# Fourier mixing and squared-ReLU MLP on one core: mirrored columns of the first sequence joined in the second block, small tables on ScalarE's queue, another order of folding and products

## The chip, the cores and the metric

The kernel runs on one core of a Trainium2 chip. The metric is the time of one execution on the device in microseconds; lower is better. It is given as the median of several runs, and one further execution is recorded by the hardware profiler.

## The reference, cut to what matters

```python
# x: (8, 3008, 256) float32; w_in: (256, 2048), w_out: (2048, 256)
X = np.fft.fft(np.fft.fft(x, axis=1), axis=2).real      # along the sequence, then along the features
h = X.reshape(24064, 256) @ w_in
g = np.maximum(h, 0.0) ** 2
out = g @ w_out
```

There are eight sequences of 3008 rows. Each goes through a two-dimensional Fourier transform whose real part is kept, and then through a two-layer network with a squared ReLU between the layers.

## The kernel before, in words

**The two halves of the work.** The transform along the features is folded into the first weight matrix: `G1` (cosines times `w_in`) and `G2` (sines times `w_in`) are made once, piece by piece, by `begin_win` and the two matmuls of L315. What is left per sequence is the transform along its 3008 rows. It gives two matrices with one column per frequency, `Pt` (cosine part) and `Qt` (sine part), and a row `Et` for the one feature column that fits in neither. The main loop then walks over blocks of 251 frequencies (`CK`) and, within a block, over eight steps `j`: `front` multiplies `Pt` and `Qt` by `G1` and `G2` (L838, L839), joins them on VectorE (L841, L843, L844), `combine` squares on ScalarE, and `back` multiplies by `w_out`. The first eight steps (the first block) also convert the weights, the second eight make sums of `w_out` (`sum_wout`). From step 8 on GpSimd forms sums for `back`.

**The first sequence** has no earlier steps to hide in, so it is transformed in a first phase ahead of the loop, in an order written out by hand. That phase is what the change is about. Its stages:

- *Load.* Seven tiles `xt` of the input (numbers 0 to 6) and the tables `cosT` and `sinT` come from memory. Tiles 0 and 1 use small tables of 95 columns, tiles 2 and 3 small tables of 189 columns, tiles 4 to 6 (`ODD0` on) large ones of 377 columns for each parity. A small table takes several DMAs. `load_table` and `load_x` issue all of these on SP's queue. `load` brings a piece of `w_in` or `w_out` as raw 64-bit words.
- *Fold.* VectorE folds each tile in two halves: `for_p(t)` (L485, L501, L515) for the cosine part, `for_q(t)` (L489, L505, L515) for the sine part. `for_p` also has ScalarE copy one column into `lone` (`f_e`, L518), which lies in the buffer `wsum`.
- *Products.* TensorE multiplies the folded tiles by the tables (L632). There are three kinds, each for both parities `kp`: P (`w` by `cosT`, into `Pt`), E (`lone` by `cosT`, for the lone column) and Q (`w` by `sinT`); E and Q add into the same PSUM tiles. The products of tiles 0 to 3 are called even, those of 4 to 6 odd.
- *Join.* ScalarE copies a part of the even products out of PSUM (`copy_4`, L650, tile `da`), and VectorE joins them in two rounds (`join_4`, `join_2`) and then with the odd products: `join_lo` gives frequencies 0 to 752, `join_hi` the mirrored ones, 753 to 1504. `join_1` does both. For Q and E these joins are the ones of L669 and L671.
- *Hand over.* `spread_e` takes the last row of `Qt` and spreads its first 251 values over all partitions by a matmul (L816); `spread_rest` does the other 1254 by two DMAs on GpSimd's queue. `copy_e` scales a column of `G2` to `gE`.

`awake(n)` issues n matmuls (L228) on a spare tile `filled`, whose result nobody uses.

**What sets the order.** The kernel is written under a manual schedule: every engine works through its own instructions in the order in which the code issues them. Each transfer issued by SP or ScalarE raises one of eight counters when it has landed. [...]

Of the kernel before, what the change touches and what calls it, by code (L numbers as in the profile page):

```python
# [8 lines left out]
F32 = mybir.dt.float32  # L9
U32 = mybir.dt.uint32  # L10
AF = mybir.ActivationFunctionType
ALU = mybir.AluOpType
# [70 lines left out]
def kernel(  # L83
# [108 lines left out]
    G2 = const.tile([P, F], F32, name="G2")  # L192
    gE = const.tile([P, NFC], F32, name="gE")

    def load_table(tab, src, tiles):

        for t in tiles:
            c, r0, step, rows = TILES[t]
            for i, (s0, count) in enumerate(row_tiles(S)):
                mine = [r for r in range(count) if (s0 + r - r0) % step == 0 and 0 <= (s0 + r - r0) // step < rows]  # L200
                if mine:
                    o, m = (s0 + mine[0] - r0) // step, len(mine)
                    while m % 15 and m % 16 and o + m < P and mine[0] + step * m < P:
                        m += 1
                    nk = NC[0][c]
                    nc.sync.dma_start(out=tab[o:o + m, :, PLACE[t]:PLACE[t] + nk],  # L206
                                     in_=src[mine[0]:mine[0] + step * (m - 1) + 1:step, :, i, 0:nk])

    make_identity(nc, ident)
    last = ident[:, P - 1:]  # L210
# [394 lines left out]
    def dft_ops(b):  # L605
# [7 lines left out]
        def group(kp, which):  # L613
# [6 lines left out]
            def product(ps, c, lone_e=False, only=None):  # L620

                ts = [t for t in range(NT) if TILES[t][0] == c]
                for t in ts if only is None else ts[only:only + 1]:
                    rows = TILES[t][3]
                    if b is None:
                        w = we[0:rows, SPOT[t], kp]
                    elif lone_e:
                        w = lone[0:rows, 2 * t + kp]
                    else:
                        w = folded[b, t][0:rows, kp, PART[which]]  # L630
                        w = w if which else w[:, 0:n]
                    nc.tensor.matmul(ps[0:w.shape[-1]], w,  # L632
                                     (cosT if lone_e else tab)[0:rows, kp, PLACE[t]:PLACE[t] + NC[kp][c]],
                                     start=t == ts[0] and (lone_e or not both_in), stop=t == ts[-1] and not lone_e,
                                     skip_group_check=both_in)
# [12 lines left out]
            def copy_4():  # L648
                a = st["a"] = hp.tile([P, 2 * P], F32, name="da", tag="da", bufs=2)[0:n]
                nc.scalar.copy(a[:, 0:n2], st["ps"][0:n, 0:n2])  # L650

            def even_part(c, lone_e):

                if c == 0 and lone_e == both_in:
                    pool, tag = (psm, ("mC", "mD")[kp]) if both_in else (psd, "d")
                    st["ps"] = pool.tile([P, 512], F32, name="pd", tag=tag)
                at, nk = EVEN[c][1:]
                product(st["ps"][:, at:at + nk], c, lone_e)
                if c == 2 and not lone_e:
                    copy_4()  # L660

            def both(lo, hi, a, ps, only=None):

                nk, nh = a.shape[-1], hi.shape[-1]
                if both_in:

                    join = nc.vector.scalar_tensor_tensor
                    if only != 1:
                        join(out=lo, in0=ps, scalar=signs[:, 0:1], in1=a, op0=ALU.mult, op1=ALU.add)  # L669
                    if only != 0:  # L670
                        join(out=hi[:, ::-1], in0=a[:, 0:nh], scalar=signs[:, 1:2], in1=ps[:, 0:nh],  # L671
                             op0=ALU.mult, op1=ALU.add)
                    return
                tt(out=lo, in0=a, in1=ps, op=ALU.add)
                if which == 1:
                    tt(out=hi[:, ::-1], in0=ps[:, 0:nh], in1=a[:, 0:nh], op=ALU.subtract)
                else:
                    tt(out=hi[:, ::-1], in0=a[:, 0:nh], in1=ps[:, 0:nh], op=ALU.subtract)

            def join_4():  # L680
                a, ps = st["a"], st["ps"]
# [2 lines left out]

            def join_2():
                a, ps = st["b"], st["ps"]
                st["c"] = hp.tile([P, NC[0][3]], F32, name="dc2", tag="dc2", bufs=2)[0:n, 0:n0]
                both(st["c"][:, 0:n1], st["c"][:, n1:n0], a, st["half"] if b != 0 else ps[:, 2 * n2:2 * n2 + n1])

            def odd_part(i, lone_e):  # L690
# [93 lines left out]
                     st["odd"], only)  # L784

            if b == 0:
                named = [("join_4", join_4), ("join_2", join_2), ("lo", join_lo), ("hi", join_hi),
                         ("join_1", join_1)]
                for i in range(3):
                    for nm, f in (("even", even_part), ("odd", odd_part)):  # L790
                        named += [(nm + ("", "_e")[e] + str(i), lambda i=i, e=e, f=f: f(i, e == 1)) for e in range(2)]
                return [((which, kp, nm), f) for nm, f in named]
            ops = [(0.0, even_n), (0.5, join_4), (0.7, join_2), (0.0, odd_n), (1.1, join_1)]
            from_psum.update((join_4, join_2, join_turned))
# [21 lines left out]
        nc.tensor.matmul(ps, last.to_broadcast([P, P]), qt[:, 0:CK], start=True, stop=True)  # L816
        nc.scalar.copy(et[:, 0:CK], ps)

    def spread_rest():
        _, qt, et = PQE[0]  # L820
        nc.gpsimd.dma_start(out=e_dram[0:1], in_=qt[P - 1:P])
        nc.gpsimd.dma_start(out=et[:, CK:], in_=e_dram[0:1, CK:].to_broadcast([P, NKT - CK]))

    def load_e(b):
        nc.sync.dma_start(out=PQE[b][2], in_=e_dram[b:b + 1].to_broadcast([P, NKT]))
# [184 lines left out]
    def for_p(t):  # L1010
        for i in (0, 2, 4):
            pieces[t][i]()
# [18 lines left out]
        product()  # L1031


    start()
    awake(48)
    for t in range(2):
        load_x(0, t)
    for_p(0)
    for_q(0)
    for_p(1)  # L1040
    begin_win(0)
    load_x(0, 2)
    load_x(0, 3)
    for dst, src in ((cosd, cos_d), (sind[:, :, 0:P - 1], sin_d), (sind[:, :, P - 1:], alt_d)):
        nc.sync.dma_start(out=dst, in_=src.rearrange("(c p) m -> p c m", p=P))
    load_table(cosT, cos_s, (0, 1))
    load_x(0, 4)
    load_x(0, 5)
    load_table(cosT, cos_s, (2, 3))
    load_x(0, 6)  # L1050
    load_table(cosT, cos_s, range(ODD0, NT))
    load_table(sinT, sin_s, range(ODD0, NT))
    win[1] = load(pair_in(1))
    load_table(sinT, sin_s, range(ODD0))
    win[2] = load(pair_in(2))
    for_p(2)
    rounded(0)
    win[0][1]()
    awake(2)
    for_p(3)  # L1060
    p_part("even0", "even1")
    q_part("even_e0", "even_e1")
    awake(6)
    p_part("even2")
    q_part("even_e2")
    for_q(1)
    for_p(4)
    for_p(5)
    for_q(2)
    for_p(6)  # L1070
    p_part("odd0", "odd1", "odd2")
    q_part("odd_e0", "odd_e1", "odd_e2")
    groups[0, 0, "join_4"]()
    groups[0, 0, "join_2"]()
    for_q(4)
    groups[0, 1, "join_4"]()
    groups[0, 1, "join_2"]()
    for_q(5)
    p_part("join_1")
    for_q(6)  # L1080
    q_part("odd0", "odd1", "odd2")
    copy_e = win[0][2]()
    begin_win(1)
    for_q(3)
    q_part("even0", "even1", "even2")
    awake(12)
    rounded(1)
    for kp in range(2):
        for nm in ("join_4", "join_2", "lo"):
            groups[1, kp, nm]()  # L1090
        if kp == 0:
            begin_win(2)
    spread_e()
    q_part("hi")
    copy_e()
    spread_rest()
    LAG = 2
    BLOCKS = [(k0, min(CK, NKT - k0)) for k0 in range(0, NKT, CK)]
    steps = [(b, k0, n, j) for b in range(B) for k0, n in BLOCKS for j in range(NJ)]
# [75 lines left out]
    for i in range(len(steps) + LAG + 4):  # L1175
        if i < len(steps):
            b, k0, n, j = steps[i]
            if i == NJ:
                for k in range(NX):
                    load_later(k)  # L1180
            if NJ <= i < NJ + NL:
                load_column(i - NJ)
            if i % per == 0:
                assert not side
                side = ahead(b + 1) if b + 1 < B else []
                spent, pace = 0.0, sum(t for t, _ in side) / sum(share(i + k) for k in range(per - 2))
            multiply()
            g = front(b, k0, n, j, between)
            if i < NJ:
                weights()  # L1190
                s = combine(n, g, True)
            elif i < 2 * NJ:
                if j < 4:
                    sum_wout(slice(j // 2 * (NJ // 2), (j // 2 + 1) * (NJ // 2)), j % 2)
        while finished and finished[0][0] <= i:
            store(*finished.pop(0)[1:])
        if i >= LAG and flight:
            at, g_, s_ = flight.pop(0)
            final = at[:3] == (B - 1, *BLOCKS[-1])
            back(at[2], at[3], g_, s_, final)  # L1200
            if at[3] == NJ - 1:
                c_ = gather(at[2], s_ is None, final)
                finished += [(i + 2 + s, *at[:3], s, c_, final) for s in range(2)]
        if i < NJ:
            copy_e = win[i + 1][2]() if i + 1 < NJ else None
            leftover()
            if copy_e:
                copy_e()
        if i < len(steps):
            flight.append(((b, k0, n, j), g, s if i < NJ else combine(n, g, False)))  # L1210
# [63 lines left out]
```

## Time and profile before

| | |
|---|---|
| median of 3 runs | 1921.69 us (1921.37 to 1922.04) |
| profiled execution, its own time | 1921.49 us |
| its span from first to last instruction | 1919.7 us |
| TensorE busy | 1908.8 us, 99% of the span |
| VectorE, GpSimd, ScalarE busy | 1444.8, 1121.0, 952.5 us |
| first matmul of the main loop (L838) | starts at 43.24 us |
| DMA moved before 33 us | 7.27 MB on SP's queue |

The span begins with the first instruction. All times below count from there. The first phase ends where L838 first appears in TensorE's timeline; all else is the loop. A duration on TensorE is that of a group in the timeline, in which each float32 matmul shows as two instructions.

### The profile page before, as it was taken

How to read it: one execution, taken by the hardware profiler on the slowest of the kernel's cores; microseconds unless marked ns; L12 is line 12 of the kernel's file. 1: busy time of each engine (PE TensorE's matmuls, PEld its weight loads, DVE VectorE, ACT ScalarE, POOL GpSimd, SP SyncE). 2: the span in 40 equal slices, each digit the busy share in tenths (PEclk: the TensorE clock that was granted, in tenths of full speed). 3: DMA queues.
4: the chain of work that ended last, by engine and by line, in shares of the span. 5: the costliest groups of instructions: out<-in, count | busy, mean ns of one | idle time of the engine just before them, and what ended most of it. 6: DMA issues, size and time to landing. Idle time of an engine off the chain costs nothing.

```text
span 1919.7 us, 28162 instructions
## 1 busy us (share of the span) xinstructions
PE 1908.8 (99%) x9270; PEld 1699.7 (89%) x9270; DVE 1444.8 (75%) x3646; ACT 952.5 (50%) x1201; POOL 1121.0 (58%) x1709
## 2 busy tenths in 40 slices
PE   9999999999999999999999999999999999999998
PEld 7888898888988898888988889888898888988887
DVE  8988887787687876788668876788767777655554
ACT  2755554555454554445545454455544555444444
POOL 0255655665566655665666665556655666566565
PEclk9999999999999999999999999999999999999999
DMA  7431211110011101111011100111001101100100
GB/s 213 129 33 33 54 30 36 28 42 17 28 36 41 34 12 35 30 45 28 12 36 42 41 21 12 47 36 36 22 20 45 36 12 22 28 12 12 22 11 23
DMA packets 146622, 69.58 MB, mean 36 GB/s; under 512 B 130145, under 2 KB 137259, under 8 KB 146474
## 3 DMA queue, kind: packets, MB, share of 16 engines
q1 hardware_dynamic: 146022, 66.87, 14.1%
q8 instruction: 73, 1.20, 0.3%
q14 instruction: 75, 0.61, 0.1%
q0 software_dynamic: 176, 0.65, 0.1%
q10 hardware_dynamic: 276, 0.26, 0.0%
HBM read 43.03 MB, written 24.69 MB: 35 GB/s over the span
## 4 chain that ended last, share of the span: by engine, by line
PE 96%; DVE 2%; DMA 1%; SPq 0%; ACT 0%; issue 0%; POOL 0%; DVEq 0%; ACTq 0%
PE ph L838 17%; PE ph L839 17%; PE mC L891 16%; PE mA L891 16%; PE mB L891 16%; PE mD L891 8%; PE pd L740 1%; PE pd L632 1%; PE mA L878 1%; PE mB L878 1%; PE pd L714 1%; DMA xt<-in_x_dram 1%; DMA cosT<-in_cos_s_dram 0%; PE pg L315 0%; SPq L206 0%
## 5 line engine op out<-in xcount | busy, mean ns | idle before, releaser
L853 ACT ACTIVATE g<-g 128x1004 f32<-128x1004 f32 (+1 forms) x384 | 399.0, 1039 | 691.8 <-DVE g L844 453.5
L841 DVE SCALAR_TENSOR_TENSOR he<-Et,gE,ph 128x251 f32<-128x251 f32 (+1 forms) x768 | 362.6, 472 | 343.2 <-PE ph L839 338.8
L861 POOL TENSOR_TENSOR s<-g 128x251 f32<-128x251 f32 (+1 forms) x376 | 236.7, 630 | 636.6 <-ACT g L854 576.7
L838 PE MATMUL ph<-Pt,G 128*128 128x251 f32 (+1 forms) x1536 | 452.5, 375 | 0.4 <-DVE g L844 0.3
L839 PE MATMUL ph<-Qt,G 127*128 127x251 f32 (+1 forms) x1536 | 451.3, 374 | 0.0
L854 ACT ACTIVATE g<-g 128x1004 f32<-128x1004 f32 (+1 forms) x384 | 399.3, 1040 | 12.2
L891 PE MATMUL mC<-s,wsum 128*128 128x251 f32 (+1 forms) x1504 | 381.4, 374 | 0.0
L891 PE MATMUL mA<-g,wout 128*128 128x251 f32 (+1 forms) x1504 | 380.1, 374 | 0.0
L843 DVE TENSOR_TENSOR g<-he,ph 128x251 f32<-128x251 f32 (+1 forms) x768 | 320.4, 417 | 53.5 <-POOL s L861 1.4
L839 PEld LDWEIGHTS ph<-Qt,G 127*128 127x128 f32 x1536 | 291.3, 190 | 35.7
L891 PEld LDWEIGHTS mC<-s,wsum 128*128 128x128 f32 x1504 | 285.5, 190 | 34.5
L838 PEld LDWEIGHTS ph<-Pt,G 128*128 128x128 f32 x1536 | 285.5, 189 | 34.5 <-DVE g L844 0.8
L844 DVE TENSOR_TENSOR g<-he,ph 128x251 f32<-128x251 f32 (+1 forms) x768 | 314.1, 409 | 0.0
L891 PEld LDWEIGHTS mA<-g,wout 128*128 128x128 f32 x1504 | 282.6, 189 | 35.3 <-issue 0.3
L862 POOL TENSOR_TENSOR s<-s,g 128x251 f32<-128x251 f32 (+1 forms) x376 | 270.7, 720 | 29.5
L863 POOL TENSOR_TENSOR s<-g 128x251 f32<-128x251 f32 (+1 forms) x376 | 272.4, 724 | 0.0
L864 POOL TENSOR_TENSOR s<-g,s 128x251 f32<-128x251 f32 (+1 forms) x376 | 241.9, 643 | 0.0
L891 PE MATMUL mB<-g,wsum 128*128 128x251 f32 (+1 forms) x752 | 220.5, 374 | 0.0
L891 PE MATMUL mD<-s,wout 128*128 128x251 f32 (+1 forms) x752 | 220.3, 374 | 0.0
L891 PE MATMUL mB<-s,wout 128*128 128x251 f32 (+1 forms) x752 | 219.9, 374 | 0.0
L891 PEld LDWEIGHTS mB<-g,wsum 128*128 128x128 f32 x752 | 142.6, 190 | 17.4
L891 PEld LDWEIGHTS mD<-s,wout 128*128 128x128 f32 x752 | 141.9, 189 | 17.7
(176 smaller groups left out, 1387.6 us busy)
## 6 DMA issues: line engine op xcount, KB each, us to landing
out_dram<-os SPq DMA_DIRECT2D x376, 56.0 KB
xt<-in_x_dram SPq DMA_DIRECT2D x39, 384.0 KB
xt<-in_x_dram SPq DMA_DIRECT2D x63, 128.0 KB
Et<-e_dram SPq DMA_DIRECT2D x7, 752.5 KB
out_dram<-os SPq DMA_DIRECT2D x288, 6.8 KB
raw<-in_moe_w_in_dram SPq DMA_DIRECT2D x16, 256.0 KB
raw<-in_moe_w_out_dram SPq DMA_DIRECT2D x16, 256.0 KB
xt<-in_x_dram SPq DMA_DIRECT2D x2, 512.0 KB
```

The lines of the kernel that those rows point to most:

```text
L838: nc.tensor.matmul(hP, G1[:, fs], pt[:, ks], start=True, stop=True)
L839: nc.tensor.matmul(hQ, G2[0:P - 1, fs], qt[0:P - 1, ks], start=True, stop=True)
L841: nc.vector.scalar_tensor_tensor(out=t, in0=et[:, ks], scalar=gE[:, fc:fc + 1], in1=hP, op0=ALU.mult, op1=ALU.add)
L843: tt(out=g[:, h, 0, 0:n], in0=t, in1=hQ, op=ALU.add)
L844: tt(out=g[:, h, 1, 0:n][:, ::-1], in0=t, in1=hQ, op=ALU.subtract)
L853: act(v, v, AF.Relu)
L854: act(v, v, AF.Square)
L861: gt(out=s1, in0=g21, in1=g22, op=ALU.add)
L862: gt(out=s2, in0=s1, in1=g11, op=ALU.subtract)
L863: gt(out=s3, in0=g11, in1=g21, op=ALU.subtract)
L864: gt(out=s4, in0=g12, in1=s2, op=ALU.subtract)
L891: nc.tensor.matmul(acc[nm][:, i, 0:n], w, v[:, 0:n], start=j == 0 and i == 0, stop=j == NJ - 1, skip_group_check=True)
```

## The change

1. `load_table` takes a queue. The small tables of `cosT` (tiles 0 to 3) and `sinT` (tiles 0 to 3) are issued by ScalarE, in three places of its order; the large ones stay on SP, which issues all seven tiles of the input ahead of them. A one-element copy on ScalarE stands first.
2. The order of folds and products is new: the P products of tiles 0 and 1 come ahead of the first `G1`/`G2` matmuls, with `awake(26)` between; the E products of tiles 5 and 6 and the Q products come later. Before the hand-over stands `awake(24)` in place of `awake(12)`.
3. Only `join_lo` is done in the first phase. `keep` copies the odd products of P and Q out of PSUM on ScalarE, into tiles of the pool `wp`, and the four `join_hi` run in steps 8 to 11, one a step.
4. The second conversion of `w_in` (`begin_win(1, True)`) has its last product on GpSimd and not on VectorE.
5. The row of `Et` is spread in two parts: frequencies 251 to 752 early on GpSimd's queue (`spread_lower`), the rest in steps 9 and 11 by SP (`store_upper`, `load_upper`).

```diff
 
-    def load_table(tab, src, tiles):
+    def load_table(tab, src, tiles, queue=nc.sync):
...
-                    nc.sync.dma_start(out=tab[o:o + m, :, PLACE[t]:PLACE[t] + nk],
-                                     in_=src[mine[0]:mine[0] + step * (m - 1) + 1:step, :, i, 0:nk])
+                    queue.dma_start(out=tab[o:o + m, :, PLACE[t]:PLACE[t] + nk],
+                                    in_=src[mine[0]:mine[0] + step * (m - 1) + 1:step, :, i, 0:nk])
...
-            def even_part(c, lone_e):
+            def even_part(c, lone_e, only=None):
...
-                product(st["ps"][:, at:at + nk], c, lone_e)
-                if c == 2 and not lone_e:
-                    copy_4()
+                product(st["ps"][:, at:at + nk], c, lone_e, only)
...
-                tt(out=lo, in0=a, in1=ps, op=ALU.add)
+                if only != 1:
+                    tt(out=lo, in0=a, in1=ps, op=ALU.add)
+                if only == 0:
+                    return
...
+            def held_w():
+                return wp.tile([P, 2, D], F32, name="w", tag="w").rearrange("p a d -> p (a d)")[0:n, 0:n0]
+
+            def keep():
+                o = held_w()
+                nc.scalar.copy(o, st["odd"])
+                st["odd"] = o
+
...
-                st["c"] = hp.tile([P, NC[0][3]], F32, name="dc2", tag="dc2", bufs=2)[0:n, 0:n0]
+                st["c"] = held_w() if both_in else hp.tile([P, NC[0][3]], F32, name="dc2", tag="dc2", bufs=2)[0:n, 0:n0]
...
         nc.scalar.copy(et[:, 0:CK], ps)
 
-    def spread_rest():
+    KH = S // 4 + 1
+
+    def spread_lower():
         _, qt, et = PQE[0]
-        nc.gpsimd.dma_start(out=e_dram[0:1], in_=qt[P - 1:P])
-        nc.gpsimd.dma_start(out=et[:, CK:], in_=e_dram[0:1, CK:].to_broadcast([P, NKT - CK]))
+        nc.gpsimd.dma_start(out=e_dram[0:1, 0:KH], in_=qt[P - 1:P, 0:KH])
+        nc.gpsimd.dma_start(out=et[:, CK:KH], in_=e_dram[0:1, CK:KH].to_broadcast([P, KH - CK]))
+
+    def store_upper():
+        nc.sync.dma_start(out=e_dram[0:1, KH:], in_=PQE[0][1][P - 1:P, KH:])
+
+    def load_upper():
+        nc.sync.dma_start(out=PQE[0][2][:, KH:], in_=e_dram[0:1, KH:].to_broadcast([P, NKT - KH]))
...
+    def folds_of(names):
+        for nm in names.split():
+            (for_p if nm[0] == "P" else for_q)(int(nm[1:]))
+
+    def products_of(names):
+        for nm in names.split():
+            (p_part if nm[0] == "P" else q_part)({"P": "", "Q": "", "E": "e"}[nm[0]] + nm[1:])
+
     start()
     awake(48)
-    for t in range(2):
-        load_x(0, t)
-    for_p(0)
-    for_q(0)
-    for_p(1)
+    load_x(0, 0)
+    load_x(0, 1)
+    nc.scalar.copy(turn[0:1, 0, 0:1], ident[0:1, 0:1])
+    load_table(cosT, cos_s, (0, 1), nc.scalar)
+    folds_of("P0 Q0 P1")
     begin_win(0)
     load_x(0, 2)
     load_x(0, 3)
     for dst, src in ((cosd, cos_d), (sind[:, :, 0:P - 1], sin_d), (sind[:, :, P - 1:], alt_d)):
         nc.sync.dma_start(out=dst, in_=src.rearrange("(c p) m -> p c m", p=P))
-    load_table(cosT, cos_s, (0, 1))
-    load_x(0, 4)
-    load_x(0, 5)
-    load_table(cosT, cos_s, (2, 3))
-    load_x(0, 6)
+    for t in range(ODD0, NT):
+        load_x(0, t)
+    load_table(cosT, cos_s, (TWO, TWO + 1), nc.scalar)
     load_table(cosT, cos_s, range(ODD0, NT))
+    win[1] = load(pair_in(1))
     load_table(sinT, sin_s, range(ODD0, NT))
-    win[1] = load(pair_in(1))
-    load_table(sinT, sin_s, range(ODD0))
     win[2] = load(pair_in(2))
-    for_p(2)
+    folds_of("Q1 P2")
     rounded(0)
+    products_of("P0 P1")
+    awake(26)
     win[0][1]()
-    awake(2)
-    for_p(3)
-    p_part("even0", "even1")
-    q_part("even_e0", "even_e1")
-    awake(6)
-    p_part("even2")
-    q_part("even_e2")
-    for_q(1)
-    for_p(4)
-    for_p(5)
-    for_q(2)
-    for_p(6)
-    p_part("odd0", "odd1", "odd2")
-    q_part("odd_e0", "odd_e1", "odd_e2")
-    groups[0, 0, "join_4"]()
-    groups[0, 0, "join_2"]()
-    for_q(4)
-    groups[0, 1, "join_4"]()
-    groups[0, 1, "join_2"]()
-    for_q(5)
-    p_part("join_1")
-    for_q(6)
-    q_part("odd0", "odd1", "odd2")
+    products_of("E0 E1")
+    folds_of("P3")
+    load_table(sinT, sin_s, range(ODD0), nc.scalar)
+    products_of("P2 P3")
+    p_part("copy")
+    products_of("E2 E3")
+    folds_of("P4 P5 Q2 P6 Q3 Q4")
+    products_of("P4 P5 P6 E4 Q0 Q1 Q2 Q3")
+    for nm in ("join_4", "join_2", "lo"):
+        groups[0, 0, nm]()
+    folds_of("Q5")
+    for nm in ("join_4", "join_2", "lo"):
+        groups[0, 1, nm]()
+    p_part("keep")
+    q_part("copy")
+    products_of("E5 E6 Q4 Q5")
     copy_e = win[0][2]()
-    begin_win(1)
-    for_q(3)
-    q_part("even0", "even1", "even2")
-    awake(12)
-    rounded(1)
-    for kp in range(2):
-        for nm in ("join_4", "join_2", "lo"):
-            groups[1, kp, nm]()
-        if kp == 0:
-            begin_win(2)
+    begin_win(1, True)
+    folds_of("Q6")
+    products_of("Q6")
+    awake(24)
+    for nm in ("join_4", "join_2"):
+        groups[1, 0, nm]()
+    halves, product, _ = win[1][0]
+    halves()
+    product()
+    for nm in ("join_4", "join_2"):
+        groups[1, 1, nm]()
+    q_part("lo")
+    copy_e()
     spread_e()
-    q_part("hi")
-    copy_e()
-    spread_rest()
+    begin_win(2)
+    q_part("keep")
+    spread_lower()
...
                 if j < 4:
                     sum_wout(slice(j // 2 * (NJ // 2), (j // 2 + 1) * (NJ // 2)), j % 2)
+                    groups[j < 2, j % 2, "hi"]()
+                    if j % 2:
+                        (store_upper if j == 1 else load_upper)()
```

More of the change, by code (lines that the diff above doesn't have):

```diff
@@ L786, in group @@
             if b == 0:
[L787 to L791, printed above, removed]
+                named = [("copy", copy_4), ("join_4", join_4), ("join_2", join_2), ("lo", join_lo), ("keep", keep),
+                         ("hi", join_hi)]
+                for e in range(2):
+                    for t in range(NT):
+                        c = TILES[t][0]
+                        f = odd_part if c == 3 else even_part
+                        args = (t - ODD0, e == 1) if c == 3 else (c, e == 1, t - TWO if c == 2 else None)
+                        named.append((("", "e")[e] + str(t), lambda f=f, args=args: f(*args)))
                 return [((which, kp, nm), f) for nm, f in named]
```

## Prediction, made before the changed kernel ran

> **What bounds the kernel now.** I read the page first. TensorE is busy nearly all of the span, so the loop is TensorE's and only time in which TensorE does not run loop work can be won or lost:
>
> ```profile
> PE 1908.8 (99%) x9270; PEld 1699.7 (89%) x9270; DVE 1444.8 (75%) x3646; ACT 952.5 (50%) x1201; POOL 1121.0 (58%) x1709
> ```
>
> The change lies in the first phase, which ends at the first L838. TensorE's timeline gives that moment and what stands before it:
>
> ```profile
> 1.37 13.58 PE L228 MATMUL filled<-ident 128*128 128x128 f32 x96 [1.37 <-POOL ident masks.py:199]
> ...
> 28.13 3.96 PE L632 MATMUL pd<-cosT,wsum 128*128 128x377 f32 x12
> 31.93 3.96 PE L632 MATMUL pd<-sinT,w 128*127 128x377 f32 x12
> 35.73 0.50 PE L324 MATMUL pe<-ident,G 128*128 128x1 f32 x4
> 36.09 2.42 PE L632 MATMUL pd<-sinT,w 95*127 95x95 f32 x16
> 38.35 2.84 PE L228 MATMUL filled<-ident 128*128 128x128 f32 x24
> 42.72 0.69 PE L816 MATMUL pe<-Qt,ident 128*128 128x251 f32 x2 [1.53 <-DVE Qt L669]
> 43.24 0.59 PE L838 MATMUL ph<-Pt,G 128*128 128x251 f32 x2
> ```
>
> The fillers L228 end (41.1) before L816 may start, so here they cost nothing: L816 waits for VectorE's joins. The chain of waits, cut to the first phase, says what was late before that:
>
> ```profile
> 16.05 1.34 SPq L206
> 17.44 9.21 DMA cosT<-in_cos_s_dram
> 26.66 0.14 issue
> 26.79 9.10 PE pd L632 x28
> ```
>
> The last large cosine table lands at 26.66; products and joins follow. After 43.24 VectorE is busy almost without gaps to the first `back` at 57.48, so a shift of the first L838 goes through to the end.
>
> Third, the waits of SP's own queue, first 60 us:
>
> ```profile
> SPq L206 <- DMA cosT<-in_cos_s_dram: 3.8, 4, 1.6
> SPq L206 <- DMA sinT<-in_sin_s_dram: 3.5, 3, 1.5
> SPq L206 <- DMA xt<-in_x_dram: 2.7, 2, 1.4
> ```
>
> An issue waits for a landing that it has no data from: the eight counters. SP's timeline shows the result, `22.98 10.93` for ten small sine tables, 1.1 us each. On SP nothing but loads stood behind them.
>
> [...] The trace before has one issuer only, so it shows just that the 16 are full (busy share 1.04 from 13 to 30 us, 272 GB/s). [...] The trace shows the cold half at the start, 12 fillers' instructions in 2 us before 7 us and 21 after it; [...]
>
> **The change, part by part.**
>
> *Small tables on ScalarE, the deciding part.* In the built program's order ScalarE has, after the copies to `G1` and `G2`: `f_e` of tile 3, ten DMA issues of small sine tables, the two `da` copies, `f_e` of tiles 4, 5, 6. The ten issues wait in this order for counters last given to: `win[1]`'s first half, the first and the third large sine table, `win[2]`'s first half, a first half of the *fourth* `w_in` piece, nothing new, that piece's second half, nothing new, the first half of a `w_out` piece, nothing new. So ScalarE passes only when that `w_out` half has landed, and behind it stand `da` (VectorE's `join_4` of P waits for it) and `f_e` of tile 4 (TensorE's E4, and in its queue all after it).
>
> When does it land? Before, 7.27 MB had moved by 33 us, through `win[1]` and most small sine tables. Up to that `w_out` half the change needs those less some 0.35 MB of small tables, plus two `w_in` pieces of 0.52 and the half of 0.26: 8.2 MB. At 265 GB/s (264 from 2 to 11 us, 272 from 13 to 30) that is 31 us after 2.0 plus 1 for the tail, 34; at the 240 GB/s of 13 to 33 us, which has the slow last engines in it, 37. The fourth piece's buffer is that of tile 4, free after its L489; VectorE would be there at about 26, so this does not decide. I take 36.3. The other nine issues are done or cost 0.43 each: two more, 37.2. Two `da` (0.24 each) and `f_e` (0.21): E4 can start at **37.8**.
>
> *Fillers and products on TensorE.* From E4 on TensorE's queue is fixed: E4 1.27 (3.80 for twelve instructions, so 0.634 a product, two of them); Q0, Q1 0.86; Q2, Q3 1.29; E5, E6 2.53; Q4, Q5 2.53; L324 0.36; Q6 1.27; together 10.1. Then 24 fillers of 0.229 (2.75 for twelve): 5.5, and now they are on the path, since L816 stands behind them. L816 0.52. Sum 16.1, first L838 at **53.9**, against 43.24: +10.7. Ahead of E4: fillers to 14.8, P0 P1 0.86, 26 fillers 5.8, `G` matmuls 1.73, E0 E1 0.9, P2 P3 and E2 E3 2.6, P4 to P6 3.8, ending near 31. TensorE would so stand idle for some 7 us and start E4 cold. The cold start lost 2.5 us (25 instructions at 0.213 instead of 0.112); [...] Nothing before shows a refall, so 0 to 2.6; I take 2.0.
>
> *VectorE's order.* Same folds. Off the path come two `join_hi` of P (0.46 each), L300 of the second piece (0.72, to GpSimd: 1.27 by the row of L298, hidden under the fillers), and the two tensor_scalars of the third piece (0.67) go behind `Qt`. All that, 2.3, I cost at nothing: VectorE stands waiting for `da`; from `da` at 37.5 it needs some 11.5 us to the low joins (two folds 3.2, P joins 3.2, conversion 1.9, Q joins 3.3), 49, earlier than the fillers' end. Without that cover it would be up to 4.4 us (rival 2).
>
> *Mirrored joins in steps 8 to 11 and copies.* Four instructions of 0.46 to 0.61, 2.1 in all. VectorE idles 0.45, 0.87 and 0.50 ahead of L841 there, 1.8, and TensorE is 1.6 us behind its buffers' release: nothing; at worst 2.1 if the cover is gone. `keep`, four copies on ScalarE: 0.37 for 256 columns, so 0.5 each; two ahead of `G` in step 0, up to 0.35 there, hidden while VectorE bounds steps 0 to 2.
>
> *Queues passed.* SP: the tiles come earlier, but VectorE waited only 0.29 for them. The ten sine issues leave SP, which then asks for the later `w_in` and `w_out` pieces sooner; this is what puts them in ScalarE's way. GpSimd has two issues as before (0.70 and 0.59), fewer bytes. SP's two `Et` issues in steps 9 and 11 stand some 60 us ahead of step 24, which needs them: nothing. TensorE's own waits for tables, 0.7 in all before, I cost at nothing too.
>
> *Sum:* +10.7 + 2.0, about +12.7; I take **12.5**. On the profiled execution's own 1921.49 (span 1919.7) that is 1934.0; it stands 0.2 under the median, so 1934.2 for the median.
>
> **Rivals.**
>
> 1. *ScalarE isn't held.* If the counters were free in time, ten issues of 0.46 after the `G` copies (23.9) end at 28.5, E4 waits for P6 at 31, and L838 comes at 31 + 16.1 = 47.1: +3.9, 1925.6. For it: DMA may run faster from two queues (412 GB/s in one slice before). Against: the waits of SP show the counters at work, and 8.2 MB by 28 us would need 315 GB/s. Bytes and place would be the same; the price is the fillers alone.
> 2. *Faster: VectorE's sum decides.* 42.58 (L816's releaser ends) less 2.3 and less its waits of 2.1 (0.29, 0.40, 1.41): 38.2, -4.4, 1917.3. The mechanism is VectorE's row freed of those five instructions and of waits. It decides only if E4 starts before 23, which the 26 fillers ahead of it forbid unless they cost far less than 0.229.
> 3. *The mirrored joins also uncover 2.1 us in steps 8 to 11:* 1936.3, from the point where VectorE's lag passes 1.6 us. [...]
> 4. *The mirrored joins are not moved*: excluded by the built order, which has them after `sum_wout`.
>
> **How the numbers follow.** A measurement of this kernel can tell 0.2%, 3.84 us, from no change. Forecast 0.78; rival 1 0.12, split evenly over the bound since +3.9 lies on it; rival 2 0.03; rival 3 0.07. Slower 0.91, same 0.06, faster 0.03. Forecast's own ends: E4 at 35.5 and no cold start gives +8.4, E4 at 39.5 with 2.6 gives +15. With part of rival 1 below and rival 3 above, the range is 1927.5 to 1938.0.
>
> **What would show it.** Right: ScalarE waits for DMA at L206, `da` comes 10 us or more later than 20.93, VectorE idles some 10 us before its first P join, TensorE idles before the E product of tile 4, and L228's 24 fillers run up to L816 without a gap. The first instructions after that idle time take twice their time. Wrong: `da` before 30; L816 waiting for VectorE; a difference that appears after step 8.

## The result, and the profile after

The changed kernel takes 1935.11 us (median of 4 runs, 1932.44 to 1937.31) against 1921.53 for the kernel before on the same chip (1921.10 to 1922.04, 4 runs). The ratio is 1.0070, with a 95% interval of 1.0052 to 1.0087: slower by 13.6 us. The profiled execution is the shortest of the four, 1932.44 with a span of 1930.7 against 1919.7 before, so its trace has 11.0 us to explain.

Line numbers moved in the changed kernel: L816 is now L828, L838 and L839 are L858 and L859, L841 is L861, and VectorE's joins are L667 to L679. TensorE's timeline of the changed kernel, in the same columns as before (start, duration, instruction, and in brackets the idle time ahead of it and who ended it), shows how the first phase ends:

```profile
16.54 0.65 PE L632 MATMUL pd<-cosT,w 94*128 94x95 f32 x4 [1.64 <-DVE win L300]
17.03 6.00 PE L228 MATMUL filled<-ident 128*128 128x128 f32 x52
...
28.55 3.96 PE L632 MATMUL pd<-cosT,w 128*128 128x377 f32 x12
36.27 2.60 PE L632 MATMUL pd<-cosT,wsum 128*128 128x377 f32 x4 [3.76 <-ACT wsum L518]
...
48.27 5.52 PE L228 MATMUL filled<-ident 128*128 128x128 f32 x48
53.62 0.59 PE L828 MATMUL pe<-Qt,ident 128*128 128x251 f32 x2
54.05 0.59 PE L858 MATMUL ph<-Pt,G 128*128 128x251 f32 x2
```

The first product of the loop, which was at 43.24, is now at 54.05: 10.8 of the 11.0 us. Read the brackets: there is one long one, 3.76 us ahead of the E product of tile 4, ended by ScalarE's L518. After it every group follows the one before without idle time, through the 48 instructions of the 24 fillers up to L828. From L858 to the end the loop takes 1930.7 - 54.05 = 1876.65 us, against 1919.7 - 43.24 = 1876.46 before. So only 0.2 of the 11.0 us belongs to the loop, and with it to the mirrored joins.

ScalarE's timeline says why L518 was late (ACTq rows are DMA issues, with their waits in the duration):

```profile
25.27 10.43 ACTq L206 DMA_DIRECT2D sinT<-in_sin_s_dram  x10
35.74 0.38 ACT L650 COPY da<-pd 128x95 f32<-128x95 f32 x2 [10.47 <-DMA sinT<-in_sin_s_dram]
36.00 0.41 ACT L518 ACTIVATE wsum<-w 128x2 f32<-128x2 f32 x3
```

Before, the first copy to `da` was made 14.8 us earlier, as soon as its product was there:

```profile
20.93 0.24 ACT L650 COPY da<-pd 128x95 f32<-128x95 f32 x1 [3.74 <-PE pd L632]
```

Ten issues of small sine tables take 10.43 us, and the copies to `da` and the three columns for the E products stand behind them. The waits of the first 62 us list the same stall three times, each on another engine, as engine, line, who was waited for, us in total, times and longest:

```profile
ACT da L650 <- DMA sinT<-in_sin_s_dram: 10.5, 1, 10.5
...
DVE db L673 <- ACT da L650: 8.9, 1, 8.9
...
PE pd L632 <- ACT wsum L518: 3.8, 1, 3.8
```

The chain of waits, cut to the window from 24 to 56 us, joins them into one path and shows what held the issues:

```profile
25.55 0.61 DVE fd L489
...
26.18 6.44 DMA raw<-in_moe_w_in_dram
...
32.64 0.32 ACTq L206
...
35.25 0.45 ACTq L206
...
35.74 0.38 ACT da L650 x2
36.12 0.11 ACT wsum L518
...
36.27 10.44 PE pd L632 x36
```

A sine table needs nothing of `w_in`. What ties them together is in the program: each of the ten sine issues names one counter in the trace, which it waits for and then raises, and the issues of SP and ScalarE up to here use eight counters (100 to 105, 109 and 110). The fifth has counter 100, as has half a `w_in` piece that SP issued at 26.18 and that landed at 32.62; it starts at 32.64. The second, third and fourth (103, 105, 109) start at 27.10, 30.47 and 31.35, each 0.02 us after the landing of what had their counter before: two sine tables at 27.08 and 30.45, half a `w_in` piece at 31.33. From the fifth on, six issues ran one after the other, 3.1 us. Then come products (10.44 and the rest), fillers, and L858.

A profile also has the granted clock of TensorE, by stretches: length, then busy time and instructions of PE, PEld, DVE, ACT and POOL, then the clock, the DMA share and GB/s. In the changed kernel:

```profile
33.00:36.30 3.30, 0.03 (x1) 0.03 (x1) 0.29 (x2) 0.56 (x5) 0.00 (x0) 1.00 0.57 153
36.30:38.30 2.00, 2.00 (x4) 1.20 (x5) 1.86 (x5) 0.58 (x3) 0.00 (x0) 0.57 0.19 46
...
40.30:44.00 3.70, 3.70 (x17) 2.71 (x16) 3.51 (x10) 2.74 (x6) 0.00 (x0) 1.00 0.54 154
```

TensorE idles from about 32.5 to 36.27; the clock falls to half at 36.60, just after E4 has begun, and is back at 40.01. Before, these stretches have 1.00, as in this one:

```profile
36.30:38.30 2.00, 2.00 (x16) 2.00 (x16) 0.59 (x2) 0.24 (x1) 0.00 (x0) 1.00 0.88 278
```

### The profile page after: what moved, and what is told of

It reads as the page before. It is cut to its first block, busy times and chain, and to the rows that moved or that the text cites. A ratio compares the mean times of both kernels' runs of the same rounds, so it can differ in the third digit from the quotient of the medians.

```text
span 1930.7 us, 28296 instructions
## 1 busy us (share of the span) xinstructions
PE 1916.5 (99%) x9330; PEld 1707.2 (88%) x9330; DVE 1444.1 (75%) x3645; ACT 954.5 (49%) x1207; POOL 1123.4 (58%) x1710
## 4 chain that ended last, share of the span: by engine, by line
PE 96%; DVE 2%; DMA 1%; ACT 0%; issue 0%; ACTq 0%; SPq 0%; POOL 0%; DVEq 0%
PE ph L858 17%; PE ph L859 17%; PE mC L911 16%; PE mA L911 16%; PE mB L911 16%; PE mD L911 8%; PE pd L749 1%; PE pd L632 1%; PE mA L898 1%; PE mB L898 1%; PE pd L723 1%; PE pg L315 0%; DMA cosd<-in_cos_d_dram 0%; DMA raw<-in_moe_w_in_dram 0%; PE filled L228 0%
## 5 line engine op out<-in xcount | busy, mean ns | idle before, releaser
L861 DVE SCALAR_TENSOR_TENSOR he<-Et,gE,ph 128x251 f32<-128x251 f32 (+1 forms) x768 | 362.4, 472 | 347.2 <-PE ph L859 337.5
L858 PE MATMUL ph<-Pt,G 128*128 128x251 f32 (+1 forms) x1536 | 452.5, 375 | 0.4 <-DVE g L864 0.3
L859 PE MATMUL ph<-Qt,G 127*128 127x251 f32 (+1 forms) x1536 | 451.3, 374 | 0.0
L859 PEld LDWEIGHTS ph<-Qt,G 127*128 127x128 f32 x1536 | 291.3, 190 | 35.7
L858 PEld LDWEIGHTS ph<-Pt,G 128*128 128x128 f32 x1536 | 285.5, 189 | 34.5 <-DVE g L864 0.8
L911 PEld LDWEIGHTS mD<-s,wout 128*128 128x128 f32 x752 | 141.9, 189 | 17.7
```

Source lines behind the costliest of these rows:

```text
L858: nc.tensor.matmul(hP, G1[:, fs], pt[:, ks], start=True, stop=True)
L859: nc.tensor.matmul(hQ, G2[0:P - 1, fs], qt[0:P - 1, ks], start=True, stop=True)
L861: nc.vector.scalar_tensor_tensor(out=t, in0=et[:, ks], scalar=gE[:, fc:fc + 1], in1=hP, op0=ALU.mult, op1=ALU.add)
L911: nc.tensor.matmul(acc[nm][:, i, 0:n], w, v[:, 0:n], start=j == 0 and i == 0, stop=j == NJ - 1, skip_group_check=True)
```

## The experiments

The theory has three terms: ScalarE is held by the ten issues (and TensorE and VectorE with it), TensorE goes cold in the idle time (it then ran at half clock for 3.41 us), and the 24 fillers lie on the path behind. The main rival is that the mirrored joins or the other order cost the time. Times are medians; ratios go by all runs and not by the medians, and are to the kernel before on the same chip. The first matmul of the loop is read from the trace, which is of one execution.

### The changed kernel once more

No edit.

> The changed kernel once more, for a second trace of it (its runs so far lie at 1932.4, 1933.2, 1937.0 and 1937.3 us). Theory (ScalarE is held by ten issues of small sine tables): the first L858 again comes 17 to 18 us after ScalarE's f_e of tile 4, and a slower execution differs in when the w_out half lands that releases ScalarE, or in how long TensorE runs cold after its idle time (at most some 2.6 us). Rival (the loop got longer by the mirrored joins): a slower execution differs after step 8.

1934.85 us, span 1933.1. ScalarE's issues end at the same place and E4 starts at 36.29, yet the loop starts 2.4 us later than in the first trace, at 56.44:

```profile
56.44 0.59 PE L858 MATMUL ph<-Pt,G 128*128 128x251 f32 x2
```

The stretches show the difference:

```profile
36.30:38.30 2.00, 2.00 (x3) 1.17 (x4) 1.86 (x5) 0.60 (x3) 0.00 (x0) 0.50 0.22 49
...
40.30:44.00 3.70, 3.70 (x13) 3.41 (x13) 3.50 (x10) 1.23 (x4) 0.00 (x0) 0.50 0.53 146
```

The clock was still at half from 40.3 to 44, where the first trace had 1.00. In this execution the half clock was on record from 34.3 us for 10.24 us, in the first from 36.6 for 3.41. The cold start is the part of the cost that varies: from E4 to L858 it took 17.78 us in one and 20.15 in the other, more than the 2.6 us that were expected at most for it. From L858 to the end it is 1876.66 us, as in the first.

### The ten issues back on SP

```diff
     load_table(sinT, sin_s, range(ODD0, NT))
+    load_table(sinT, sin_s, range(ODD0))
     win[2] = load(pair_in(2))
...
     folds_of("P3")
-    load_table(sinT, sin_s, range(ODD0), nc.scalar)
     products_of("P2 P3")
```

> One part of the change undone: the small sine tables go back to SP's queue, behind the large ones; all else as changed. Theory (ScalarE held, then fillers on the path): ScalarE's da copies come near 29 us instead of 35.7, E4 follows P6 without idle time at about 32.4, no cold stretch, first L858 at 32.4 + 16.1 = 48.5 instead of 54.05, time about 1927, still some 5 above the kernel before because the 24 fillers stay. Rival A (only the fillers cost, ScalarE's wait is covered): no change, 1932 to 1935. Rival B (the mirrored joins cost it in the loop): no change.

1925.60 us (1924.71 to 1929.02, 7 runs), ratio 1.0024 (1.0013 to 1.0035). ScalarE comes to `da` as soon as its product is there, and TensorE runs from P6 into E4 with no gap:

```profile
29.32 3.96 PE L632 MATMUL pd<-cosT,w 128*128 128x377 f32 x12
33.12 1.43 PE L632 MATMUL pd<-cosT,wsum 128*128 128x377 f32 x4
...
49.11 0.59 PE L858 MATMUL ph<-Pt,G 128*128 128x251 f32 x2
```

E4 is 3.15 us earlier, and from E4 to L858 it takes 15.99 us instead of 17.78, with the clock at 1.00 in every stretch from 30 to 44 us: 4.94 together. This shows the first two terms. The loop starts at 49.11 and not at 48.5 as expected, because the products of P6 end later than in the changed kernel.

### Two fillers in place of 24

```diff
     products_of("Q6")
-    awake(24)
+    awake(2)
```

> One number changed: 2 fillers ahead of the hand-over instead of 24; ScalarE still issues the small sine tables. Theory: L828 no longer stands behind fillers but waits for VectorE's low joins, which end at 49.0 in the trace of the changed kernel; L828 at 49.2 instead of 53.6, so 4.4 us less, about 1928. Rival A (fillers alone explain the loss): back to 1923 or less. Rival C (ScalarE alone, fillers hidden as in the kernel before): no change.

1928.46 us (1927.54 to 1931.55, 5 runs), ratio 1.0037 (1.0024 to 1.0051). ScalarE is held as in the changed kernel, E4 comes at 36.71, and the end of the phase is:

```profile
48.69 0.61 PE L228 MATMUL filled<-ident 128*128 128x128 f32 x4
49.55 0.69 PE L828 MATMUL pe<-Qt,ident 128*128 128x251 f32 x2 [0.26 <-DVE Qt L667]
50.08 0.59 PE L858 MATMUL ph<-Pt,G 128*128 128x251 f32 x2
```

The loop starts 4.0 us earlier, with E4 0.4 later: 4.4. The 22 fillers taken out were 4.9 us long (24 took 5.36); the bracket tells where half of the rest is, since L828 now waits for VectorE's join of `Qt`. The fillers did lie on the path, with little to spare behind them.

### Both

The two edits above together.

> Both of the last two edits. Theory: the two add up but for what VectorE and TensorE's products still need: first L858 at 43.5 to 44.5, 1921.5 to 1923, level with the kernel before. Rival B (loop): stays 2 us or more above the kernel before with a first L858 as early as before.

1922.57 us (1920.64 to 1924.79, 12 runs), ratio 1.0004 (0.9995 to 1.0013): no difference from the kernel before that can be told. The end of the phase:

```profile
44.47 0.69 PE L828 MATMUL pe<-Qt,ident 128*128 128x251 f32 x2 [0.26 <-DVE Qt L667]
44.99 0.59 PE L858 MATMUL ph<-Pt,G 128*128 128x251 f32 x2
```

The terms add: the two edits alone moved L858 by 4.94 and 3.97, both together by 9.06. What is left to the 43.24 of before is 1.75 us, for everything else in the change.

### The mirrored joins alone

The order and queues of the kernel before, and of the change only parts 3 and 5: `join_lo` and `keep` in the first phase, the four `join_hi` in steps 8 to 11, `Et` in two parts.

```diff
-    p_part("join_1")
+    p_part("lo"); p_part("keep")
...
+                    groups[j < 2, j % 2, "hi"]()
+                    if j % 2:
+                        (store_upper if j == 1 else load_upper)()
```

> One part of the change alone: the kernel before with its own order, loads and fillers, but with the four mirrored joins moved to steps 8 to 11, the four copies that this needs and the Et row in two parts. Theory: the two P joins leave VectorE at a place where TensorE's odd products end later anyway (VectorE stood idle 0.40 and 1.41 us after them), the two Q joins stood behind L816 beside TensorE: no gain. In steps 8 to 11 they lie beside TensorE: no loss. First L838's counterpart within 0.5 us of 43.24, time 1921 to 1922. Rival B (the joins cost in the loop): 2 us more, 1923.7, with an unchanged first phase. Rival D (they are the gain that was lost elsewhere): 2 us less or better, 1919.5.

1921.76 us (1920.49 to 1925.43, 20 runs), ratio 1.0007 (1.0000 to 1.0013). The rival falls: the joins cost 0.7 us by the medians, 1.3 by the ratio and 2.5 at the end of its interval, of 13.6. They also bring nothing, though they take two `join_hi` from VectorE's path. Part of the 1.3 is the clock: the record has the mean granted clock of every run, and the eight runs with 1.000 have a median of 1921.1, against 1921.04 for the kernel before, while the seven with 0.997 or 0.998 have 1923.9. In the 38 runs of the kernel before beside them it is never below 0.999; why it falls more often here was not tested. In the profiled execution, 1924.35, the loop starts at 45.23, not within 0.5 us of 43.24 as expected, and the clock fell twice in it, at 25.18 and 45.66:

```profile
24.24 5.73 PE L632 MATMUL pd<-cosT,w 128*128 128x377 f32 x12 [1.82 <-DVE w L515]
29.81 3.96 PE L632 MATMUL pd<-cosT,wsum 128*128 128x377 f32 x12
```

Two groups of the same twelve instructions, 5.73 us against 3.96: 0.94 us after the first began, the clock fell to half for 3.41 us. The idle time ahead of the group was 1.82 us.

### The ten issues on ScalarE alone

The kernel before, with one edit.

```diff
-    load_table(sinT, sin_s, range(ODD0))
...
     awake(6)
+    load_table(sinT, sin_s, range(ODD0), nc.scalar)
```

> Another part alone: the kernel before, with nothing changed but that the ten small sine tables are issued by ScalarE, ahead of the P products of tiles 2 and 3, and not by SP. Theory: ScalarE is held there too, though for less, since the counters it waits for belong to the tables and to the second and third w_in piece: da near 29 us instead of 20.9, the first P join and E4's counterpart late, first L838 at 47 to 48.5, 1925.5 to 1927. Its 12 fillers stay hidden. Rival A (only fillers cost) and rival E (a second issuing engine helps, since SP's ten issues of 1.1 us go): no change or less, 1921 or lower.

1925.66 us (1924.61 to 1926.30, 9 runs), ratio 1.0025 (1.0016 to 1.0035). ScalarE's timeline has the same picture in another order of work:

```profile
17.62 11.06 ACTq L206 DMA_DIRECT2D sinT<-in_sin_s_dram  x9
28.72 0.38 ACT L650 COPY da<-pd 128x95 f32<-128x95 f32 x2 [11.42 <-PE pd L632]
```

and TensorE's has the loop's start:

```profile
46.75 0.59 PE L838 MATMUL ph<-Pt,G 128*128 128x251 f32 x2
```

The bracket names TensorE because its product was the last thing that `da` needed by the records; ScalarE was in fact busy issuing up to 28.68. `da` is 7.8 us later than the 20.93 of before and the loop starts 3.5 later. Most of the rest is slack that VectorE had: its first P join came at 23.50 before, 2.6 us after `da`, and is at 28.99 now; and its later waits of 0.40 and 1.41 us are gone. The move is costly by itself, without the new order.

### TensorE kept busy over the stall

In the changed kernel, 16 matmuls of `ident` into a part of E's tile that nobody reads, between P6 and E4. They are meant to fill the idle time, with E4 still waiting for ScalarE.

```diff
+            def warm():
+                for _ in range(16):
+                    nc.tensor.matmul(st["full"][:, 3 * P:], ident, ident, start=True, stop=True)
...
-    products_of("P4 P5 P6 E4 Q0 Q1 Q2 Q3")
+    products_of("P4 P5 P6")
+    groups[0, 1, "warm"]()
+    products_of("E4 Q0 Q1 Q2 Q3")
```

> The changed kernel with 16 more fillers between P6 and E4, written into unused columns of a PSUM tile (3.6 us of TensorE work in the 3.8 to 4.5 us in which it stands idle). Theory: with that idle time filled TensorE's clock doesn't fall to half, E4 starts when ScalarE lets it, near 36.3, and L858 follows 16.1 us later at 52.4 to 52.9 instead of 54.05 and 56.5; time 1930.5 to 1931.5, and the runs lie closer together than the 1932.4 to 1937.3 of the changed kernel. Rival F (the slow stretch after the wait is something else, such as tables that land late): no gain, or 3.6 us more where the fillers stand on the path.

1931.91 us (1931.35 to 1935.13, 4 runs), ratio 1.0061 (1.0048 to 1.0075). Three runs are at 1931.4 to 1931.9, under the shortest run of the changed kernel, 1932.44; their mean granted clock is 0.999 to 1.000, where every run of the changed kernel has 0.997 or 0.998. The profiled one is the fourth, 1935.13 with 0.998, and shows another case: the clock had fallen at another place: to half at 17.7 us, during the early wait of 2.81 us ahead of P1, and back at 24.5.

```profile
18.47 1.14 PE L632 MATMUL pd<-cosT,w 94*128 94x95 f32 x4 [2.81 <-DMA cosT<-in_cos_s_dram]
19.40 8.44 PE L228 MATMUL filled<-ident 128*128 128x128 f32 x52
...
37.16 3.73 PE L691 MATMUL pd<-ident 128*128 128x128 f32 x32
40.73 1.43 PE L632 MATMUL pd<-cosT,wsum 128*128 128x377 f32 x4
```

The 26 early fillers took 8.44 us where they take 6.00 at full clock, so the products of P6 ended only at about 37.2. ScalarE was free of its issues by then and copied `da` at 37.14. The 16 fillers (L691) thus filled no idle time here: E4 stood behind them, some 3 us. From E4 on TensorE ran with the clock at 1.00: E4 took 1.43 us instead of 2.60, and from E4 to the fillers ahead of the hand-over it was 10.2. The loop started at 56.73, not at 52.4 to 52.9 as expected. So the clocks of the other three runs speak for a cold start that was taken away, but no trace of one of them was kept, and the intervals of this run and of the changed kernel overlap (1.0048 to 1.0075, 1.0052 to 1.0087); the size of the gain isn't settled.

### Another order, to beat both kernels

The changed kernel with all sine tables on SP and ahead of the second `w_in` piece, the 26 early fillers cut to two, the 24 late ones to two, the products of P0 and P1 and tile 3's fold ahead of `rounded(0)`, the rest of the first conversion of `w_in`, the Q products of tiles 0 to 3 after all E products, and Q6's fold ahead of the second conversion. The main lines of the edit:

```diff
-    awake(26)
+    awake(2)
...
-    products_of("P4 P5 P6 E4 Q0 Q1 Q2 Q3")
+    products_of("P4 P5 P6 E4")
...
-    products_of("E5 E6 Q4 Q5")
+    products_of("E5 E6 Q0 Q1 Q2 Q3"); q_part("copy"); products_of("Q4 Q5")
...
-    awake(24)
+    awake(2)
```

> A version made from the findings: small sine tables on SP behind the large ones, the second w_in piece loaded after them, 2 fillers in place of 26 and of 24, the G matmuls after P0 P1 and tile 3's fold, E5 and E6 ahead of Q0 to Q3, the second conversion after the fold of Q6. Theory: the DMA engines become the bound of the first phase (they have 7.3 MB to bring by about 33 us in any order), so little is left to win: L858 at 42 to 43, 1920.3 to 1921.5, at most 1 us better than the kernel before. Rival G (what is left is VectorE's row): L858 at 40 or earlier, 1918.5 or less.

1921.26 us (1917.79 to 1923.41, 13 runs), ratio 0.9998 (0.9990 to 1.0006): no difference. But five runs lie from 1917.8 to 1919.0 and seven from 1921.3 to 1923.4, with one between. The profiled execution is of the upper kind, 1922.38; its clock was at half from 22.6 us for 6.83, and its loop started at 44.23, later than the 42 to 43 that were expected. The mean granted clock separates the two kinds: 0.997 or 0.998 in six of the seven upper runs and 0.999 in the other, 0.999 or 1.000 in the five lower ones.

### The same, with fillers where TensorE waited

```diff
-    products_of("P0 P1")
+    products_of("P0")
+    awake(7)
+    products_of("P1")
...
-    products_of("P2 P3")
+    awake(4)
+    products_of("P2")
+    awake(4)
+    products_of("P3")
```

> The reordered kernel of the run before, with 15 of the idle matmuls L228 put where its TensorE waited ahead of the large cosine tables: seven between the products of P0 and P1, four ahead of P2 and four ahead of P3. In the reordered kernel's profiled execution the granted clock fell to half at 22.6 us, after waits of 1.82, 0.76 and 1.09 us, and the runs fell into two groups, near 1918.5 and near 1922. If the groups are that fall, and short waits bring it on, then with the waits filled the clock stays at one in the profiled execution and most runs lie near the lower group, 1918 to 1919.5, 0.1% under the kernel before. If the groups come from when the transfers land, the fillers change nothing, and the median stays at 1921 to 1922. If the fillers are late themselves (15 times 0.229 is 3.4 us, into 3.7 us of waiting), the products of tiles 4 to 6 start later than 27.4 us and it is slower, 1922 to 1923.

1920.02 us (1918.53 to 1924.33, 21 runs), ratio 0.9992 (0.9985 to 0.9998). The mean granted clock is 1.000, and the P products of tiles 4 to 6 come at 26.11, 1.33 us earlier than in the run before and at full rate. In the run before they were

```profile
27.44 4.97 PE L632 MATMUL pd<-cosT,w 128*128 128x377 f32 x12
```

and here the first phase goes on like this:

```profile
26.11 3.96 PE L632 MATMUL pd<-cosT,w 128*128 128x377 f32 x12
29.91 3.96 PE L632 MATMUL pd<-cosT,wsum 128*128 128x377 f32 x12
...
41.38 0.69 PE L828 MATMUL pe<-Qt,ident 128*128 128x251 f32 x2 [0.65 <-DVE Qt L667]
41.90 0.59 PE L858 MATMUL ph<-Pt,G 128*128 128x251 f32 x2
```

L858 is at 41.90, 2.3 us earlier than in the run before it and 1.3 earlier than in the kernel before, and the median is 1.55 us (0.08%) under the kernel before: a small gain, its interval clear of one. The two groups are gone, 18 of 21 runs lie from 1918.5 to 1920.7. Most were expected at 1918 to 1919.5 and only 8 came there, so the fall of the clock explains the upper group but not all of the spread. These runs are on another chip, where the kernel before is 0.5 us slower (1921.57 against 1921.04), which is part of the shift. What makes the rest stays open.

## Why the prediction was right, by its own steps

The prediction was 1934.2 us, and 1935.1 was measured. The sign and the mechanism held; some terms of the sum were off and partly cancelled. That the total lies so near is in part luck: E4 came 1.5 us earlier than put, and the cold start cost up to 2.2 us more.

**ScalarE held: right, 1.5 us too long.** E4 was put at 37.8 and came at 36.27. The step that was off is the landing that lets ScalarE pass. The prediction named the counters in the right order and had the last of them held by half a `w_out` piece until 36.3. By the trace that half landed at 34.01, before its counter was asked for at 34.77, so it held nobody. The last real wait was on the first half of the fourth `w_in` piece, landed at 32.62; from there on six issues took 3.1 us, where the prediction had two and 0.9. The bytes were sized by a rate that was too low. The 240 GB/s takes in 30 to 33 us of the kernel before, and there the DMA engines were not slow but had little to do (busy share 0.21); in the changed kernel 13 to 33 us have 274 GB/s. The 265 GB/s that the same paragraph worked out first gave 34, the measured landing. The prediction also said that the buffer's release by VectorE's L489 doesn't decide. The chain runs through it, at 26.16. As the DMA engines were nearly full up to 33 us (share 0.99 from 30 to 33), an earlier release may not have helped; that wasn't tried.

**P products: 1.5 us late, at no cost.** The prediction had them end near 31 and TensorE idle for 7 us. They ended at 32.5 and it idled 3.76. The failed step is "TensorE's own waits for tables, 0.7 in all before, I cost at nothing too": P1 waited 1.64 us. The bracket names VectorE's L300, but that ended at 16.02, half a microsecond before P1 began at 16.54. The last DMA of the small cosine tables landed at 16.45. In the traces with the issues back on SP, with both edits and with TensorE kept busy P1 also begins 0.09 us after that landing, so the table is what it waited for; it is one of those that ScalarE issues. E4 was later still, so this hid in the idle time. Without the stall it counts: rival 1 put the loop's start at 47.1, and the run with the issues back on SP has 49.11, with 1.84 us of waiting ahead of P1.

**From E4 to the loop: right.** 16.1 was the sum; with the clock at one it measured 15.99, and the fillers' part, 5.5, measured 5.36.

**Cold start: right in the profiled execution, too narrow as a bound.** 2.0 was taken, with 0 to 2.6 as ends. Against 15.99 the first trace lost 1.8, the second 4.2. Half of the time on record at half clock while TensorE worked is 1.7 us in the first (3.41) and 4.15 in the second (8.3 of the 10.24), so this is nearly all of the loss. That the clock would fall in the idle time was the author's estimate: after the start the trace before shows no fall (1.00 in every stretch from 7 us on). The bound allowed for no more than the 2.5 us that the fillers lost at the start, and in the second trace TensorE worked for 8.3 us without a gap before the clock was back at one. The longer cold stretch is also the likely reason why the median stands 13.6 us above the kernel before and the profiled execution only 11.0: the two runs at 1937 have a mean granted clock of 0.997, as the second trace has, and the two at 1932.4 and 1933.2 have 0.998. No trace of a run at 1937 exists.

**VectorE's order: right.** Low joins were put at 49, and `gE` behind the last of them starts at 48.99; idle time before the first P join was put at some 10 us and was 8.87. The cover was thin: with 22 fillers gone L828 waited 0.26 us for it.

**Mirrored joins: right.** Nothing in the loop (+0.19 us of 1876), and alone at most a small cost (ratio 1.0000 to 1.0013), part of which is the clock.

**The rivals.** Rival 1 (ScalarE isn't held) falls with the 10.43 us; what it priced is what the kernel with the issues on SP does: its median, 1925.6, is the price named, partly by luck, since the start is 2.0 us later than it said. Its hope for a faster DMA from two queues wasn't met: 13 to 30 us moved 264 GB/s, against 272 before. Rival 2 (VectorE's sum decides) would have needed E4 before 23. Rival 3 (joins uncovered) falls with the loop's 0.19.

Put together, of the 10.81 us by which L858 moved: 3.15 ScalarE's hold and 1.79 the cold start (the issues back on SP), 4.12 the fillers (both edits against that), and 1.75 for all else. How much of the last term the early fillers and the later cosine table stand for is not shown: P products of tiles 4 to 6 start at 29.59 with both edits and at 26.11 in the last run, which changed several things at once.

## What to carry to other kernels

A DMA issue wasn't free here to the engine that made it. The issues share eight counters in this program, so the second to fifth of the ten waited for transfers that they had nothing to do with (the fifth for half a `w_in` piece, up to 32.62 us), and so did all compute behind them on ScalarE (10.43 us for ten issues). Back on SP, with nothing but loads behind them there, the ten left E4 3.15 us earlier. To put the issues behind the engine's last urgent instruction may serve as well, but wasn't tried here. And fillers were free only while something else ended later: before, they ended at 41.1 with L816 at 42.72; in the changed kernel they lay on the path (taking out 22 of 24 gained 4.1 to 4.4 us). Place them in the waits that the trace shows, and look again after every change of order.

## What was not expected of the hardware

The prediction reckoned with a cold start after some 7 us of idle time. On record the granted clock fell with shorter waits too. These are the waits of TensorE ahead of each fall in the first phase, and the longest ones of three traces without a fall:

| trace | idle time of TensorE, us | granted clock |
|---|---|---|
| changed kernel, first | 3.76, up to 36.27 | half from 36.60 |
| changed kernel, second | 4.26, up to 36.29 | half from 34.3 |
| two fillers in place of 24 | 4.51, up to 36.71 | half from 37.3 |
| TensorE kept busy | 2.81, up to 18.47 | half from 17.7 |
| joins alone | 1.82, up to 24.24 | half from 25.18 |
| joins alone | 1.84, up to 44.70 | half from 45.66 |
| another order | 1.82, 0.76 and 1.09, up to 16.59, 21.57 and 23.54 | half from 22.6 |
| issues back on SP | 1.84, up to 17.30 | no fall |
| both edits | 2.31, up to 17.57 | no fall |
| kernel before | 1.53, up to 42.72 | no fall |

So in these traces the length of a gap doesn't decide it: the clock fell with one of 1.82 us and not with one of 2.31. What does decide it is not shown.

Nor is it shown why the same program lost 1.8 us once and 4.2 the other time. What differs on record is this: in the first trace the clock fell 0.33 us after E4 had begun and was back 3.41 us later; in the second it fell at 34.3, while TensorE still stood idle, and stayed at half through 8.3 us in which TensorE worked without a gap.
